# Talking-heads attention before two dense networks: four PSUM banks and an earlier place for the premix, scores in two banks one pair of heads a step

## The chip, the cores and the metric

The kernel runs on one NeuronCore of a Trainium2 chip. TensorE (PE in the rows) multiplies matrices into PSUM, VectorE (DVE), ScalarE (ACT) and GpSimd (POOL) work beside it, and SyncE (SP) issues the transfers, which 16 DMA engines carry out. The metric is the time of one execution on the device in microseconds (us), the median of several.

## The reference

Everything is float32. The attention mixes the heads twice, before and after the softmax; then come two dense networks.

```python
def _attn_ref(q, k, v, w_pre, w_post):            # q, k, v: (4, 12, 448, 64)
    scores = (1 / sqrt(64)) * matmul(q, k^T)      # (4, 12, 448, 448)
    scores = einsum('bhij,hg->bgij', scores, w_pre)
    scores = scores - max(scores, axis=-1)
    attn = exp(scores)
    attn = attn / (sum(attn, axis=-1) + 1e-09)
    attn = einsum('bhij,hg->bgij', attn, w_post)
    return matmul(attn, v)

x = attn_out.transpose(0, 2, 1, 3).reshape(1792, 768)
x = ((x @ w1) * (x @ w2)) @ w3 @ w_out            # _moe_ref
h = x @ w_in; out = maximum(0.01 * h, h) @ w_out2 # _moe2_ref
```

## The kernel before

`attention()` runs first, `moe()` after it. The attention takes, for each of the 4 batches, the 448 query rows in chunks of 120, 120, 120 and 88, and a chunk in blocks of ten rows: 12, 12, 12 and 9 blocks, 180 in all. A block's ten rows times twelve heads fill 120 partitions. This is how a block passes through:

- *Scores* (`qk`): for a pair of heads, `p`, six matmuls with queries and keys split in a high and a low half, into two PSUM banks `pq` (tag `qa`, four banks). ScalarE copies them to `s` (in the first two chunks VectorE copies one of the two), and after every second pair a transfer writes `s` to memory (`sdr`). Scores are made two chunks ahead (`QAHEAD`), in the steps listed in `QT`, two pairs a step.
- *Relayout* (`relayout`): a transfer reads a pair of blocks back as `sr`, with row and head on the partitions, eight steps ahead (`AHEAD`); there are five `sr` buffers.
- *Premix and softmax* (`premix`): for two blocks at once four matmuls mix the heads of `sr` into banks `pm` (one for each block, two in all); in the trace these are eight records. For each block VectorE takes the maximum `mx`, and ScalarE the exponential `e` with its sum.
- *Weights of the second mix* (`sums`, `weigh`): GpSimd adds 1e-9, VectorE takes the reciprocal `rc`, GpSimd scales the mixing matrix by it (`kr`), a step later.
- *Post-mix* (`postmix`): three steps later (`LAG`) four matmuls (eight records) mix `e` into `po` (two banks), and VectorE, or ScalarE in some steps, copies it to `ap`.
- *Values* (`av`): when a chunk's `ap` is full, at steps 3 and 4 of the next chunk, 24 matmuls (48 records) into `px`, a bank of tag `qa`, copied to `y` and written out.

Beside that, in steps that are not `plain` (those in `QT` or `AT`), `filler` advances: it converts a weight of the dense networks from a 64-bit format in 16 units of six calls, five operations on VectorE and two on ScalarE a unit, with one transfer in and one out. `lows` are the low halves of later queries and keys; their subtraction runs in steps 3 and 4 on VectorE, behind the post-mix's copy.

The attention is under a manual schedule: every engine gets its instructions in the order in which the loop over `n` at the end of `attention()` calls these functions, one step for each `n`, and runs them in that order. In a step this is: stores of the step before (`flush`), premix and softmax, `weigh`, `sums`, `relayout`, scores, `av`, post-mix, `lows`, filler. A PSUM tile of a tag takes the tag's banks in turn and waits until the one it gets has been read.

Of the kernel before, what the change touches and what calls it, by code (L numbers as in the profile page):

```python
# [23 lines left out]
def attention_moe_kernel(ctx: ExitStack, tc, qt, kt, vt, w_pre, w_post, w1, w2, w3t, w_out, w_in2, w_out2, out):  # L24
# [20 lines left out]
    HP = 2  # L45
# [21 lines left out]
    make_identity(nc, ident)  # L67

    ps = ctx.enter_context(tc.tile_pool(name="ps", bufs=2, space=PSUM))
    banks = {"qa": 4, "pm": 2, "po": 2}  # L70

    def bank(tag, shape, name):
        return ps.tile(shape, F32, tag=tag, name=name, bufs=banks[tag])
# [45 lines left out]
    def attention():  # L119
        with ExitStack() as es:  # L120
# [78 lines left out]
            def qk(b, c, p):  # L199

                m = cols[c]
                g, r = divmod(p, HP)
                first = (b, c) == order[0]
                if first and p == 0:
                    st[b, c] = late.tile([CH, H, S], F32, tag="ap", name="s", bufs=2)
                elif not first and r == 0:
                    st[b, c] = big.tile([CH, 2 * HP, S], F32, tag="s", name="s", bufs=4)
                t = st[b, c][:, 2 * g * HP:2 * (g + 1) * HP] if first else st[b, c]
                pq = [bank("qa", [CH, S], "pq") for _ in range(2)]
                for j, (x, y) in enumerate(((0, 0), (0, 1), (1, 0))):  # L210
                    for e in range(2):
                        rows = slice(e * D, (e + 1) * D)
                        nc.tensor.matmul(  # L213
                            pq[e][:m], qst[b, c][rows, p, x, :m], kst[b, p][rows, y, :], start=(j == 0), stop=(j == 2)
                        )
                for e in range(2):
                    if e and order.index((b, c)) < QAHEAD:
                        nc.vector.tensor_copy(t[:m, 2 * r + e, :], pq[e][:m])
                    else:
                        nc.scalar.activation(out=t[:m, 2 * r + e, :], in_=pq[e][:m], func=ACTF.Copy)  # L220
                if r == HP - 1:
                    stores.append((sdr[b, c][:, 2 * g * HP:2 * (g + 1) * HP, :], t[:m]))
# [30 lines left out]
                        nc.sync.dma_start(out=sr[s * Q:s * Q + HR, g], in_=st[b, c][q0:q0 + HQ])  # L253

            def premix(n):
                if n in srt:
                    sr = srt.pop(n)
                    for s, m, _, nb in pair_of(n):
                        pms[m] = bank("pm", [P, S], "pm")
                        rows = slice(s * Q, s * Q + nb // 2 * H)  # L260
                        for g in range(2):
                            nc.tensor.matmul(  # L262
                                pms[m][g * Q:(g + 1) * Q], kpre[rows], sr[rows, g, :], start=True, stop=True
                            )
                pm = pms.pop(n)
                mx = wk.tile([P, 1], F32, tag="mx", name="mx")
                nc.vector.tensor_reduce(out=mx, in_=pm, axis=AX.X, op=ALU.max, negate=True)  # L267
# [138 lines left out]
            for n in range(4, AHEAD):  # L406
                relayout(n)
            q_split(0, 2)()
            for n in range(NB + LAG):
                flush()  # L410
                plain = True
                if n < NB:
                    b, c, t, _ = blocks[n]
                    ci = order.index((b, c))
                    QT = (5, 8, 10) if ci == 0 else (0, 6, 9) if len(chunks[c][2]) > 9 else (0, 5, 7)
                    plain = t not in QT and t not in AT
                    premix(n)
                if 0 < n <= NB:
                    weigh(n - 1)
                if n < NB:  # L420
# [8 lines left out]
                        if c == NC - 2:  # L429
                            lows += [k_split(b + 1, p) for p in ((2, 3) if t == LAG else (4, 5))]  # L430
                    if ci + QAHEAD < len(order) and t in QT:
                        for r in range(HP):
                            qk(*order[ci + QAHEAD], HP * QT.index(t) + r)
                m = n - LAG
                if m >= 0:
                    tt = blocks[m][2]
                    if tt < 2 and m > tt:
                        av(*blocks[m - tt - 1][:2], tt)
                    postmix(m, nc.scalar.copy if n >= NB or plain and t in (1, 5, 8, 10) else nc.vector.tensor_copy)
                while lows:  # L440
                    lows.pop(0)()
                if n < NB:
# [16 lines left out]
    def moe():  # L459
        with ExitStack() as es:  # L460
# [4 lines left out]
            so = es.enter_context(tc.tile_pool(name="m_so", bufs=4, reuse_waits="tile"))  # L465
            wk = es.enter_context(tc.tile_pool(name="m_wk", bufs=2, reuse_waits="tile"))
            xp = es.enter_context(tc.tile_pool(name="m_x", bufs=1, reuse_waits="tile"))
            tags = itertools.cycle(("qa", "pm", "qa", "po"))

            def pst(shape, name):  # L470
                return bank(next(tags), shape, name)
# [219 lines left out]
```

## Time and profile before

| | us |
|---|---|
| median of 3 runs | 1470.07 |
| lowest, highest | 1465.48, 1473.9 |
| the profiled execution | 1471.89 |
| its span, first to last instruction | 1470.1 |

| share of the span | busy |
|---|---|
| TensorE matmuls | 94% |
| TensorE weight loads | 79% |
| VectorE | 59% |
| ScalarE | 42% |
| GpSimd | 10% |

The granted TensorE clock was 0.964 of full speed in the mean. The trace names the function's lines: L213 is `qk`'s matmul, L262 the premix's, L267 and L270 its maximum and exponential, L299 the post-mix's matmul, L306 its copy, L319 `av`'s matmul, L220 and L218 the copies of scores, L97 to L106 and `hl` the conversions. The attention fills the first 590 us, so views of a stretch say more than the page's totals. An engine's instructions are busy from start to end; matmuls are pipelined, so the next start is the better measure of what one costs.

### The profile page before, as it was taken

To read this page: it belongs to the slowest core of one execution; us is meant where nothing else is said; L and a number is where in the kernel's file an instruction comes from. 1 tells how busy PE (TensorE), PEld (TensorE's weight loads), DVE (VectorE), ACT (ScalarE), POOL (GpSimd) and SP (SyncE) were. 2 spreads that over 40 slices of the span, in tenths; PEclk is the share of its full clock that TensorE was granted. 3 is DMA by queue.
4 is the path that set the end of the run, shared out by engine and by line. 5 is a ranking of instruction groups with operands and counts; after the bars stand their busy time and mean duration, and the time that the engine had idled before them with its cause. 6 is when DMAs were issued, how large, how long until landed. Compare 5 with 4: busy or idle time off the path is not lost.

```text
span 1470.1 us, 23122 instructions
## 1 busy us (share of the span) xinstructions
PE 1388.4 (94%) x8880; PEld 1165.1 (79%) x8880; DVE 869.5 (59%) x1508; ACT 610.1 (42%) x1174; POOL 149.7 (10%) x371
## 2 busy tenths in 40 slices
PE   6788888898889998999999999999999999999998
PEld 3466565675566666998889899999988888999998
DVE  4344554545445456767643768687666446776962
ACT  3354555445454444533322445234333223552430
POOL 1222222222222232000000000000000000000000
PEclk8798999889889999999999999999999999999999
DMA  5965797677577687763314243242723131532401
GB/s 170 280 211 162 222 280 210 168 222 222 166 209 213 172 244 215 234 193 102 109 43 122 70 167 108 86 150 87 236 87 101 57 122 65 172 102 93 131 20 76
DMA packets 138861, 224.21 MB, mean 153 GB/s; under 512 B 20032, under 2 KB 120384, under 8 KB 138304
## 3 DMA queue, kind: packets, MB, share of 16 engines
q1 hardware_dynamic: 138752, 222.73, 50.3%
q8 instruction: 71, 1.16, 0.3%
q14 instruction: 38, 0.31, 0.1%
HBM read 162.86 MB, written 58.98 MB: 151 GB/s over the span
## 4 chain that ended last, share of the span: by engine, by line
PE 85%; DVE 5%; ACT 4%; issue 3%; DMA 2%; SPq 1%; DVEq 0%; ACTq 0%
PE pm L557 40%; PE po L626 16%; PE po L299 8%; PE pm L262 6%; PE px L319 6%; PE pq L213 5%; PE pw L495 5%; ACT e L270 3%; DVE mx L267 2%; DMA sr<-sdr 1%; DVE ap L306 1%; DMA sr<-s 1%; DVE ks L179 1%; DVE wc L103 1%; SPq L253 0%
## 5 line engine op out<-in xcount | busy, mean ns | idle before, releaser
L557 PE MATMUL pm<-x,ws 128*128 128x512 f32 (+1 forms) x2304 | 466.8, 363 | 0.0
L557 PEld LDWEIGHTS pm<-x,ws 128*128 128x128 f32 x2304 | 417.6, 188 | 47.7
L626 PE MATMUL po<-ws,g 128*128 128x384 f32 x1344 | 234.2, 334 | 0.0
L626 PEld LDWEIGHTS po<-ws,g 128*128 128x128 f32 x1344 | 233.1, 188 | 0.0
L270 ACT ACTIVATE e<-pm,mx 128x448 f32<-128x448 f32 x180 | 114.4, 635 | 254.3 <-DVE rc L282 236.0
L299 PEld LDWEIGHTS po<-kr,e 128*112 128x112 f32 x1440 | 166.9, 187 | 59.9 <-issue 31.7
L262 PE MATMUL pm<-sr,kpre 60*64 60x448 f32 x720 | 152.5, 574 | 53.6 <-ACT e L270 39.7
L299 PE MATMUL po<-kr,e 128*112 128x120 f32 (+1 forms) x1440 | 190.9, 285 | 1.8 <-ACT ap L306 1.8
L306 DVE COPY ap<-po 112x480 f32<-112x480 f32 (+1 forms) x125 | 81.4, 651 | 167.7 <-PE po L299 167.7
L79 DVE TENSOR_TENSOR ws<-wc,ws 128x768 fp32r<-128x768 f32 (+1 forms) x104 | 101.2, 975 | 76.8 <-ACT ws L76 76.4
L284 POOL TENSOR_SCALAR kr<-kpost,rc 128x120 f32<-128x120 f32 x180 | 105.7, 587 | 377.0 <-DVE rc L282 342.7
L95 ACT ACTIVATE wc<-wr 128x768 f32<-128x768 f32 (+2 forms) x120 | 104.5, 875 | 76.0 <-DVE ws L79 63.6
L76 ACT ACTIVATE ws<-wc 128x768 fp32r<-128x768 f32 (+1 forms) x104 | 89.1, 859 | 106.8 <-PE po L626 73.9
L267 DVE TENSOR_REDUCE mx<-pm 128x1 f32<-128x448 f32 x180 | 110.6, 616 | 36.3 <-PE pm L262 28.8
L262 PEld LDWEIGHTS pm<-sr,kpre 60*64 60x64 f32 x720 | 31.4, 133 | 113.7 <-ACT e L270 83.9
L557 PE MATMUL pm<-h,ws 128*128 128x512 f32 (+1 forms) x576 | 116.3, 363 | 0.0
L557 PEld LDWEIGHTS pm<-h,ws 128*128 128x128 f32 x576 | 104.3, 188 | 11.7
L319 PEld LDWEIGHTS px<-ap,vs 112*64 112x64 f32 x1536 | 91.0, 159 | 25.9 <-issue 25.1
L103 DVE SCALAR_TENSOR_TENSOR wc<-wr,wc 128x768 uint32<-128x768 uint32 (+2 forms) x120 | 109.9, 917 | 1.5
L106 DVE SCALAR_TENSOR_TENSOR wc<-wr,wc 128x768 uint32<-128x768 uint32 (+2 forms) x120 | 109.9, 916 | 1.2
L319 PE MATMUL px<-ap,vs 112*64 112x120 f32 (+1 forms) x1536 | 98.0, 294 | 12.7 <-DVE ap L306 9.0
L220 ACT ACTIVATE s<-pq 120x448 f32<-120x448 f32 (+1 forms) x180 | 84.5, 547 | 22.6 <-PE pq L213 21.8
(51 smaller groups left out, 1011.7 us busy)
## 6 DMA issues: line engine op xcount, KB each, us to landing
sr<-sdr SPq DMA_DIRECT2D x172, 210.0 KB
sdr<-s SPq DMA_DIRECT2D x36, 840.0 KB
wr<-in_moe_w_dram SPq DMA_DIRECT2D x32, 768.0 KB
wr<-in_moe_w_in_dram SPq DMA_DIRECT2D x32, 768.0 KB
wr<-in_moe_w_out_dram SPq DMA_DIRECT2D x32, 768.0 KB
wr<-in_moe_w_dram SPq DMA_DIRECT2D x8, 1024.0 KB
sdr<-s SPq DMA_DIRECT2D x12, 616.0 KB
wr<-in_moe_w_out_dram SPq DMA_DIRECT2D x16, 384.0 KB
```

Of the source, the lines that this page charges most:

```text
L79: nc.vector.tensor_tensor(out=dst, in0=src, in1=hi.bitcast(F32), op=ALU.subtract)
L95: nc.scalar.activation(out=cf, in_=hi.bitcast(F32), func=ACTF.Abs)
L103: lambda: nc.vector.scalar_tensor_tensor(out=c, in0=hi, scalar=0xC0000000, in1=c, op0=ALU.bitwise_and, op1=ALU.bitwise_or),
L106: lambda: nc.vector.scalar_tensor_tensor(out=c, in0=lo, scalar=29, in1=c, op0=ALU.logical_shift_right, op1=ALU.bitwise_or),
L262: nc.tensor.matmul(pms[m][g * Q:(g + 1) * Q], kpre[rows], sr[rows, g, :], start=True, stop=True)
L267: nc.vector.tensor_reduce(out=mx, in_=pm, axis=AX.X, op=ALU.max, negate=True)
L270: ends["act"] = nc.scalar.activation(out=e, in_=pm, func=ACTF.Exp, bias=mx, scale=1.0, accum_out=sm)
L284: ends["pool"] = nc.gpsimd.tensor_scalar(out=kr, in0=kpost, scalar1=rc, scalar2=None, op0=ALU.mult)
L299: nc.tensor.matmul(po[:, jc].rearrange("p h (g i) -> p h g i", g=2), e[:, jc * JP:(jc + 1) * JP], kr, start=True, stop=True,)
L319: nc.tensor.matmul(px[e * D:(e + 1) * D, p - p0, :ni], vst[b][:, jc, 2 * p + e, :], ap[:, jc, 2 * p + e, :ni], start=(jc == 0), stop=(jc = ...
L557: nc.tensor.matmul(dst, wt[:, a, kk, :], x[:, kk, c, c0:c0 + w], start=(kk == 0 and j == 0), stop=(kk == kn - 1 and j == 2),)
L626: nc.tensor.matmul(po, g[:, m, a, t * P:(t + 1) * P], wts[m][:, c, 0, cs], start=(m == 0 and j == 0), stop=(m == FQ - 1 and j == 2),)
```

## The change

The banks are dealt anew: `pm` gets four and `qa` two. The premix is taken apart: `premix` keeps the matmuls, and a new `softmax` has the maximum and the exponential. The matmuls of the next pair of blocks are issued at the end of an even step, behind the post-mix; the first pair's before the loop. Scores are made one pair of heads a step, in six steps of a chunk instead of three, and those of the first two chunks take `pm` banks for two pairs of three. With `QT` longer, there are more steps that are not plain: `filler` is called two times in each `QT` step, so 14 times a chunk instead of 8. The post-mix's copy is ScalarE's in all plain steps. In `moe()` the tags are dealt in another turn.

```diff
--- before.py
+++ after.py
@@ -67,7 +67,7 @@
     make_identity(nc, ident)
 
     ps = ctx.enter_context(tc.tile_pool(name="ps", bufs=2, space=PSUM))
-    banks = {"qa": 4, "pm": 2, "po": 2}
+    banks = {"qa": 2, "pm": 4, "po": 2}
 
     def bank(tag, shape, name):
         return ps.tile(shape, F32, tag=tag, name=name, bufs=banks[tag])
@@ -206,7 +206,7 @@
                 elif not first and r == 0:
                     st[b, c] = big.tile([CH, 2 * HP, S], F32, tag="s", name="s", bufs=4)
                 t = st[b, c][:, 2 * g * HP:2 * (g + 1) * HP] if first else st[b, c]
-                pq = [bank("qa", [CH, S], "pq") for _ in range(2)]
+                pq = [bank("pm" if (b, c) in order[:QAHEAD] and p % 3 else "qa", [CH, S], "pq") for _ in range(2)]
                 for j, (x, y) in enumerate(((0, 0), (0, 1), (1, 0))):
                     for e in range(2):
                         rows = slice(e * D, (e + 1) * D)
@@ -253,6 +253,7 @@
                         nc.sync.dma_start(out=sr[s * Q:s * Q + HR, g], in_=st[b, c][q0:q0 + HQ])
 
             def premix(n):
+
                 if n in srt:
                     sr = srt.pop(n)
                     for s, m, _, nb in pair_of(n):
@@ -262,6 +263,8 @@
                             nc.tensor.matmul(
                                 pms[m][g * Q:(g + 1) * Q], kpre[rows], sr[rows, g, :], start=True, stop=True
                             )
+
+            def softmax(n):
                 pm = pms.pop(n)
                 mx = wk.tile([P, 1], F32, tag="mx", name="mx")
                 nc.vector.tensor_reduce(out=mx, in_=pm, axis=AX.X, op=ALU.max, negate=True)
@@ -406,15 +409,17 @@
             for n in range(4, AHEAD):
                 relayout(n)
             q_split(0, 2)()
+            premix(0)
             for n in range(NB + LAG):
                 flush()
                 plain = True
                 if n < NB:
                     b, c, t, _ = blocks[n]
                     ci = order.index((b, c))
-                    QT = (5, 8, 10) if ci == 0 else (0, 6, 9) if len(chunks[c][2]) > 9 else (0, 5, 7)
+                    nt = len(chunks[c][2])
+                    QT = (5, 7, 8, 9, 10, 11) if ci == 0 else (0, 1, 5, 7, 9, 11) if nt > 9 else (0, 1, 2, 5, 7, 8)
                     plain = t not in QT and t not in AT
-                    premix(n)
+                    softmax(n)
                 if 0 < n <= NB:
                     weigh(n - 1)
                 if n < NB:
@@ -429,14 +434,15 @@
                         if c == NC - 2:
                             lows += [k_split(b + 1, p) for p in ((2, 3) if t == LAG else (4, 5))]
                     if ci + QAHEAD < len(order) and t in QT:
-                        for r in range(HP):
-                            qk(*order[ci + QAHEAD], HP * QT.index(t) + r)
+                        qk(*order[ci + QAHEAD], QT.index(t))
                 m = n - LAG
                 if m >= 0:
                     tt = blocks[m][2]
                     if tt < 2 and m > tt:
                         av(*blocks[m - tt - 1][:2], tt)
-                    postmix(m, nc.scalar.copy if n >= NB or plain and t in (1, 5, 8, 10) else nc.vector.tensor_copy)
+                    postmix(m, nc.scalar.copy if n >= NB or plain else nc.vector.tensor_copy)
+                if n < NB and t % 2 == 0:
+                    premix(n + len(pair_of(n)))
                 while lows:
                     lows.pop(0)()
                 if n < NB:
@@ -465,7 +471,7 @@
             so = es.enter_context(tc.tile_pool(name="m_so", bufs=4, reuse_waits="tile"))
             wk = es.enter_context(tc.tile_pool(name="m_wk", bufs=2, reuse_waits="tile"))
             xp = es.enter_context(tc.tile_pool(name="m_x", bufs=1, reuse_waits="tile"))
-            tags = itertools.cycle(("qa", "pm", "qa", "po"))
+            tags = itertools.cycle(("pm", "qa", "pm", "po"))
 
             def pst(shape, name):
                 return bank(next(tags), shape, name)
```

Three places in the engines' order. The first is TensorE in the middle of a chunk of twelve blocks, the third of the second batch, from its second `px` on (step 4). Before:

```order
L319 MATMUL px<-ap,vs 64x120 x24
L299 MATMUL po<-kr,e 112x120 x8
L262 MATMUL pm<-sr,kpre 64x448 x4
L213 MATMUL pq<-ks,qs 120x448 x12
L299 MATMUL po<-kr,e 112x120 x8
L262 MATMUL pm<-sr,kpre 64x448 x4
L299 MATMUL po<-kr,e 112x120 x4
L213 MATMUL pq<-ks,qs 120x448 x12
L299 MATMUL po<-kr,e 112x120 x4
L262 MATMUL pm<-sr,kpre 64x448 x4
```

After:

```order
L322 MATMUL px<-ap,vs 64x120 x24
L302 MATMUL po<-kr,e 112x120 x4
L263 MATMUL pm<-sr,kpre 64x448 x4
L213 MATMUL pq<-ks,qs 120x448 x6
L302 MATMUL po<-kr,e 112x120 x8
L263 MATMUL pm<-sr,kpre 64x448 x4
L213 MATMUL pq<-ks,qs 120x448 x6
L302 MATMUL po<-kr,e 112x120 x8
L263 MATMUL pm<-sr,kpre 64x448 x4
L213 MATMUL pq<-ks,qs 120x448 x6
L302 MATMUL po<-kr,e 112x120 x8
L263 MATMUL pm<-sr,kpre 64x448 x4
```

A group of twelve score matmuls has become two of six, two steps apart, and the premix, which stood a step later behind one post-mix more, follows the post-mix of an even step.

The second is ScalarE's order where one chunk ends and the next begins (88 columns: scores for a chunk of nine blocks; 120: the next). Before:

```order
L220 ACTIVATE s<-pq 88x448 x4
L270 ACTIVATE e,sm<-pm,mx 128x448
L306 COPY ap<-po 112x48x10
L270 ACTIVATE e,sm<-pm,mx 128x448 x2
L220 ACTIVATE s<-pq 120x448 x4
L95 ACTIVATE wc<-wr 128x384
L270 ACTIVATE e,sm<-pm,mx 128x448
L306 COPY ap<-po 112x48x10
```

After:

```order
L309 COPY ap<-po 112x48x10
L273 ACTIVATE e,sm<-pm,mx 128x448
L220 ACTIVATE s<-pq 88x448 x2
L76 ACTIVATE hl<-wc 128x384
L273 ACTIVATE e,sm<-pm,mx 128x448
L220 ACTIVATE s<-pq 120x448 x2
L273 ACTIVATE e,sm<-pm,mx 128x448
L220 ACTIVATE s<-pq 120x448 x2
L95 ACTIVATE wc<-wr 128x384
L273 ACTIVATE e,sm<-pm,mx 128x448
L309 COPY ap<-po 112x48x10
```

There are now score copies in three steps that follow each other, the last of a chunk and the first two of the next, each between two exponentials; before there were two steps without any between them.

The third is VectorE at the end of a chunk in the first batch, with conversions (`wc`, `hl`). Before:

```order
L306 COPY ap<-po 112x48x10
L267 TENSOR_REDUCE mx<-pm 128x1
L282 RECIPROCAL rc<-sm 128x1
L306 COPY ap<-po 112x48x10
L100 TENSOR_SCALAR wc<-wc 128x384
L103 SCALAR_TENSOR_TENSOR wc<-wr,wc 128x384
L267 TENSOR_REDUCE mx<-pm 128x1
L282 RECIPROCAL rc<-sm 128x1
L267 TENSOR_REDUCE mx<-pm 128x1
L282 RECIPROCAL rc<-sm 128x1
L306 COPY ap<-po 112x48x10
```

After:

```order
L79 TENSOR_TENSOR hl<-wc,hl 128x384
L97 TENSOR_SCALAR wc<-wc 128x384
L270 TENSOR_REDUCE mx<-pm 128x1
L285 RECIPROCAL rc<-sm 128x1
L309 COPY ap<-po 112x48x10
L100 TENSOR_SCALAR wc<-wc 128x384
L103 SCALAR_TENSOR_TENSOR wc<-wr,wc 128x384
L270 TENSOR_REDUCE mx<-pm 128x1
L285 RECIPROCAL rc<-sm 128x1
L309 COPY ap<-po 112x48x10
L106 SCALAR_TENSOR_TENSOR wc<-wr,wc 128x384
L270 TENSOR_REDUCE mx<-pm 128x1
```

Behind each `ap` of a step with scores there are now one or two conversions before the next `mx`, in steps that follow each other; before, one step of the same stretch had them.

## Rows read from the trace of the kernel before

**Rows 1.** Busy time by stretch: us, each engine's busy time (instructions), clock, DMA share, GB/s

```profile
50.00:550.00 500.00, 448.95 (x3828) 307.37 (x3827) 245.76 (x584) 246.32 (x610) 134.25 (x330) 0.92 0.74 211
...
600.00:650.00 50.00, 50.00 (x290) 50.00 (x289) 39.61 (x48) 23.85 (x36) 0.00 (x0) 1.00 0.73 236
```

**Rows 2.** TensorE by line, 50 to 550 us: count, busy and mean, idle before, releasers

```profile
L299 PE MATMUL po<-kr,e 128*112 128x120 f32 (+1 forms) x1320 | 175.3, 285 | 0.0
L262 PE MATMUL pm<-sr,kpre 60*64 60x448 f32 (+1 forms) x660 | 133.4, 564 | 39.7 <-ACT e L270 38.9
L319 PE MATMUL px<-ap,vs 112*64 112x120 f32 (+1 forms) x1344 | 88.8, 300 | 11.3 <-DVE ap L306 8.1 <-issue 3.2
L213 PE MATMUL pq<-ks,qs 64*120 64x448 f32 (+1 forms) x504 | 69.3, 412 | 0.0
```

**Rows 3.** TensorE in time: start, duration, instruction, count, idle before and its releaser

```profile
62.26 1.89 PE L299 MATMUL po<-kr,e 128*112 128x120 f32 x16
64.08 0.97 PE L262 MATMUL pm<-sr,kpre 60*64 60x448 f32 x4
66.07 0.97 PE L262 MATMUL pm<-sr,kpre 60*64 60x448 f32 x4 [1.02 <-ACT e L270]
66.97 1.48 PE L213 MATMUL pq<-ks,qs 64*120 64x448 f32 x12
68.38 1.89 PE L299 MATMUL po<-kr,e 128*112 128x120 f32 x16
...
161.33 0.98 PE L262 MATMUL pm<-sr,kpre 60*64 60x448 f32 x8
162.25 2.68 PE L319 MATMUL px<-ap,vs 112*64 112x120 f32 x48
164.86 1.07 PE L299 MATMUL po<-kr,e 128*112 128x120 f32 x8
165.86 1.47 PE L213 MATMUL pq<-ks,qs 64*120 64x448 f32 x12
```

**Rows 4.** TensorE in time after a longer wait, and the stretch's busy times and clock

```profile
266.75 1.28 PE L262 MATMUL pm<-sr,kpre 60*64 60x448 f32 x4 [1.47 <-ACT e L270]
267.97 2.60 PE L213 MATMUL pq<-ks,qs 64*120 64x448 f32 x12
...
270.00:280.00 10.00, 9.69 (x60) 6.67 (x60) 4.21 (x11) 5.58 (x15) 2.43 (x6) 0.79 0.71 191
```

**Rows 5.** All engines in time, one post-mix and what follows it

```profile
302.44 1.07 PE L299 MATMUL po<-kr,e 128*112 128x120 f32 x8
...
303.55 0.66 DVE L306 COPY ap<-po 112x480 f32<-112x480 f32 x1 [0.46 <-PE po L299]
...
304.39 0.62 DVE L267 TENSOR_REDUCE mx<-pm 128x1 f32<-128x448 f32 x1
...
305.13 0.63 ACT L270 ACTIVATE e<-pm,mx 128x448 f32<-128x448 f32 x1 [2.81 <-DVE rc L282]
...
305.75 1.83 ACT L220 ACTIVATE s<-pq 120x448 f32<-120x448 f32 x4
```

**Rows 6.** VectorE by line, 50 to 550 us: two of the conversions

```profile
L103 DVE SCALAR_TENSOR_TENSOR wc<-wr,wc 128x384 uint32<-128x384 uint32 x16 | 8.9, 556 | 0.4
...
L97 DVE TENSOR_SCALAR wc<-wc 128x384 f32<-128x384 f32 x16 | 5.6, 352 | 0.0
```

**Rows 7.** Busy time by stretch, where transfers are dense, and two lines of transfer issues

```profile
50.00:60.00 10.00, 9.60 (x58) 6.87 (x57) 4.74 (x11) 4.39 (x12) 2.86 (x8) 0.72 1.05 227
60.00:70.00 10.00, 8.98 (x67) 5.88 (x68) 4.04 (x10) 6.41 (x15) 2.63 (x7) 1.00 0.97 290
320.00:330.00 10.00, 9.26 (x129) 8.02 (x128) 4.17 (x10) 2.56 (x8) 2.17 (x6) 0.83 1.01 295
...
wr<-in_moe_w_out_dram SPq DMA_DIRECT2D x16, 384.0 KB
wos<-hl SPq DMA_DIRECT2D x16, 384.0 KB
```

## The prediction

> **What bounds the kernel now.** I read the busy time by stretch first. From 600 us on TensorE is busy for all 50 of 50 us at full clock, and that part, the two dense networks, is left alone by the change; only its bank names are dealt anew, and a bank of each name is still used again after eight tiles. So the question is the attention, some 590 us. In 500 us of it [rows 1] TensorE is busy 449 us, VectorE and ScalarE 246 each, the granted clock is 0.92 and the transfers take 0.74 of their engines. TensorE is the engine to look at, and it idles only 51 us.
>
> Then its lines in that stretch [rows 2]: 1320 matmuls of the post-mix are 165 blocks at 8 records each, so a block takes 3.03 us. 39 us of the idle time stand before the premix (`pm`), nearly all ended by ScalarE's exponential `e`, and 11 before `px`.
>
> Third, TensorE in order of time [rows 3]. The first five rows are one pair of blocks: two post-mixes start 1.82 us apart from the premix, whose first half runs 0.97 us alone, then 1.02 us of waiting for `e`, then the second half. The loop is plain: two `pm` banks hold both blocks of a pair, the next pair's premix needs them empty, and both maxima and exponentials lie between. The other rows of the group show it undisturbed: eight records together start the next work after 0.92 us. So a split premix costs 0.95 us that the profile calls busy.
>
> The Trainium skill says the same of the counter ("Perfetto Trace Analysis", Identifying the Most-Contended Engine: matmul busy time is a poor measure of the distance to the roofline). By busy time alone the change could give back 51 us at most, a time of about 1421; the sum below goes by starts in the rows instead.
>
> What the matmuls of the stretch would take end to end at full clock, from starts [rows 3] and counts [rows 2]:
> - post-mix: 165 blocks at 0.91 in twos and 1.00 alone, 0.95 taken: 157 us
> - premix: 82.5 pairs at 0.92: 76
> - scores: 504/12 = 42 groups at 1.41: 59
> - `px`: 1344/48 = 28 at 2.61: 73
>
> Together 365 us, 2.21 a block. Of the 500 us, 51 are idle. The premix is busy 133.4 us; 82.5 pairs of 0.98 would be 81, and 52 over 0.97 says that some 54 pairs ran split: 51 us. The 33 left (449 - 365 - 51) are the clock: after 1.47 us of idling the same twelve score matmuls took 2.60 us, against 1.48, with 0.79 granted in that stretch [rows 3, 4], a time spent partly at the 1.2 GHz level and otherwise at 2.4.
>
> **The change part by part.** *Premix ahead.* The premix of a pair now stands at the end of the even step before it and needs the exponentials of blocks that the other engines had two steps earlier. From the end of a post-mix to `e` is 0.04 + 0.66 (`ap`) + 0.62 (`mx`) + 0.12 + 0.62 = 2.1 us [rows 5], while TensorE has two post-mixes, a premix and mostly half a score group, over 2.7 us, before it asks. So the wait and the split go: 39 + 51 us. The premix also slips between the last post-mix and `px`, so the waits there, 11 us in all, are covered. If that cover failed, they would be paid again, nothing more. The new risk is data: the premix is now ahead of a post-mix in TensorE's queue and would hold it up if `sr` had not landed. The load is issued six to seven steps ahead instead of eight, about 17 us instead of 24. In the 500 us no idle time of size is ended by it [rows 2], so I take nothing here and put the risk with the transfers below.
>
> *Scores in two banks, a pair a step.* The work is the same, 84 steps of 6 matmuls instead of 42 of 12. What is new is that two banks hold just one pair, so each step needs ScalarE's two copies of the step before it to be done. Where a step without scores lies between, there is time enough. Where two score steps follow each other there isn't. From the end of a post-mix: 0.04, `ap` 0.66, `mx` 0.62, 0.12, `e` 0.62, two copies at 0.46 each (four took 1.83), 0.04 make 3.0 us [rows 5]. TensorE meanwhile has a premix 0.92, half a score group 0.71 and a post-mix 0.95, 2.6 in all: a wait of 0.5. With two conversion steps between `ap` and `mx`, 0.35 to 0.56 each [rows 6], 0.8 in all, the wait is 1.3 us. All that stands behind the waiting score matmul, the post-mix and then `ap`, `mx` and `e` of the next blocks, is held up too, so it costs in full. Six steps in a chunk make 36 such neighbours in 14 chunks: four in the first chunk, two in each of the others with twelve blocks, four in each with nine. 16 have conversions: 16 x 1.3 + 20 x 0.5 = 31 us. Bounds: 0 if ScalarE keeps up, and 84 x 1.3 = 109 if every step waited.
>
> *Conversions sooner.* They run in steps that have scores, now twice as many: 14 calls a chunk instead of 8, so the 98 calls are done by about block 92, not in the twelfth chunk. No work is added, but it lies on fewer blocks. At the two `px` steps of a chunk VectorE also has low halves to subtract, two operations like the 0.56 one [rows 6]; I take 0.8 us a chunk for 15 chunks, 12 us (bounds 0 and 24).
>
> *Copies.* `ap` goes to ScalarE in 52 steps instead of 55, three more VectorE copies at 0.66: 2 us on an engine half idle, nothing. *The start.* The first scores get six banks instead of four. From 50 us on the transfers are at 1.05 of their share [rows 7] and the premixes there wait for data, so I take 0 (bounds -3 and 3).
>
> *Transfers.* 211 GB/s for 500 us are 105 MB, 0.64 MB a block, of which the conversions' 16 loads and 16 stores of 384 KB are 12.6 MB. Without them 0.56 MB a block; with all of them in 78 blocks 0.73 there. The rows with a share near 1 moved 227, 290 and 295 GB/s [rows 7], 271 in the mean: 2.69 us a block. By the terms above the engines need 2.21 + 29/78 of waits + 0.12 of clock = 2.70 in those blocks, so both are at their limits together. I add 8 us for that (bounds 0 and 41, from 290 and from 227 GB/s).
>
> *Clock.* Waits fall from 51 + 51 to 31 + 12. In proportion the 33 us become 14 (bounds 0 and 33).
>
> The sum for the stretch: 365 + 31 + 12 + 14 + 8 = 430 us instead of 500, 70 less. The nine blocks behind it lose the split and the waits too (102/165 a block) but have no scores, less the 12 us kind: 3 us. The profiled execution took 1471.9 us (span 1470.1), 1.8 above the median of 1470.07, well within the runs. 1471.9 - 73 = 1399; the median lies a little lower, so I say 1398.
>
> **The rivals.**
> 1. *TensorE runs dense.* ScalarE and VectorE catch up during the two `px` steps and no score step waits; the clock then stays up. 31 + 12 + 14 + 8 fall away: 1335 to 1360. For it: both engines are busy half the time. Against it: the order on VectorE ties `mx` to the post-mix before it.
> 2. *Transfers set the pace of the first half.* At 227 GB/s a block takes 3.22 us, at 248 2.94, against 2.80 in the forecast: 11 to 33 us more, 1409 to 1431. For it: rows at a share of 1 already [rows 7]. Against it: they are bursts, and pairs are loaded many steps ahead.
> 3. *The clock doesn't recover.* The short waits before scores keep it at 0.92 and the 33 us stay: 1417. The rows bear it out so far: 1.47 us of idling was followed by a lower clock [rows 3, 4]. The Trainium skill ("TensorE: Matmul & The Clock Gate", A second HAM failure mode) describes short idle times while cycling through PSUM banks that set the clock swinging.
> 4. *No gain.* VectorE falls so far behind that the premix still waits for `e`, one step later than now: 1465 to 1478.
> 5. *Slower: the two score banks become the loop.* ScalarE's queue is late in all score steps, not only neighbours, since `ap` copies and `e` alternate with score copies there. Without score waits the sum is 1367; the time of before returns at 103/84 = 1.2 us for each of the 84 steps. With the 0.56 us lag of a late ScalarE copy added to 1.3 it is 1.9 each, 160 us: 1527. For it: no second pair of banks. Against it: in alternate steps the copies have a whole step of 2 us more.
>
> **How the numbers follow.** Forecast (1380 to 1412) 0.46; dense 0.13; transfers 0.16; clock 0.09; no gain 0.06; slower 0.10. About 0.5% is what a measurement of this kernel can tell from no change. Faster by more than that 0.84, within it 0.06, slower 0.10. The range leaves out the slower case, no gain, and the lower part of the dense case: 1352 to 1435.
>
> **What would show it.** Right: `pm` no longer waits for `e`, its busy time falls to about 80 us for as many pairs, and idle time before `pq` ended by ScalarE's score copies appears, about 30 us, at chunk ends. The first half shows a transfer share of 0.9 or more, and blocks are slower there than after the conversions. Wrong: idle time before `pm` ended by `sr` transfers (rival 2), a clock still at 0.92 (rival 3), `pq` idle over 80 us (rival 5), or hardly any (rival 1).

## The result, and the profile after

| | before | after |
|---|---|---|
| median of four runs, us | 1468.38 | 1384.45 |
| lowest to highest, us | 1465.48 to 1473.9 | 1381.86 to 1387.82 |
| the profiled execution, us | 1471.89 | 1382.40 |
| its span, us | 1470.1 | 1380.6 |

The changed kernel takes 0.9426 of the time of before (95% interval 0.9387 to 0.9464): 84 us less by the medians, 89.5 by the two profiled spans. The prediction was 1398 with a range of 1352 to 1435 and a gain of 73 us against the profiled execution.

All of it is in the attention. The first matmul of the dense networks started at 584.97 us before and starts at 495.45 now, 89.5 us earlier, which is the whole difference of the spans. The first rows are the busy time by stretch, in the columns of [rows 1]:

```profile
50.00:470.00 420.00, 398.40 (x3920) 279.07 (x3922) 254.24 (x604) 243.94 (x621) 158.61 (x342) 0.99 0.86 255
...
50.00:300.00 250.00, 234.16 (x2258) 163.82 (x2258) 160.64 (x381) 149.81 (x377) 97.88 (x192) 0.98 0.88 267
300.00:470.00 170.00, 164.24 (x1667) 115.25 (x1668) 93.60 (x224) 94.13 (x244) 60.73 (x150) 1.00 0.84 237
```

TensorE is busy 398 of 420 us where it was 449 of 500 [rows 1], the granted clock is 0.99 instead of 0.92, and the transfers are at 0.86 instead of 0.74 of their engines: much the same bytes in less time. The second and third row part the stretch near where the conversions end (the last `hl` is written at 281 us). The lines of TensorE in it, which answer [rows 2]:

```profile
L302 PE MATMUL po<-kr,e 128*112 128x120 f32 (+1 forms) x1368 | 173.6, 276 | 0.1
L263 PE MATMUL pm<-sr,kpre 60*64 60x448 f32 (+1 forms) x684 | 89.4, 561 | 0.8 <-DMA sr<-sdr 0.6
L213 PE MATMUL pq<-ks,qs 64*120 64x448 f32 (+1 forms) x504 | 81.1, 396 | 6.9 <-ACT s L220 6.3
L322 PE MATMUL px<-ap,vs 112*64 112x120 f32 (+1 forms) x1364 | 75.0, 268 | 13.8 <-ACT ap L309 12.9 <-ACT s L220 0.9
```

The premix `pm` waits 0.8 us where it waited 39.7, and none of that for `e`. Its 684 records are 85.5 pairs, 89.4 us, 1.05 us a pair; before it was 133.4 us for 82.5 pairs, 1.62. So the split is gone as well as the wait. What is idle now, 21.6 us, stands before `px` (13.8) and before the scores `pq` (6.9). TensorE in time, one end of a chunk and the next one's beginning, in the columns of [rows 3]:

```profile
97.00 1.07 PE L302 MATMUL po<-kr,e 128*112 128x120 f32 x8
98.92 1.30 PE L213 MATMUL pq<-ks,qs 64*120 64x448 f32 x6 [0.85 <-ACT s L220]
100.15 1.08 PE L302 MATMUL po<-kr,e 128*112 128x120 f32 x8
101.16 0.98 PE L263 MATMUL pm<-sr,kpre 60*64 60x448 f32 x8
102.07 0.87 PE L213 MATMUL pq<-ks,qs 64*120 64x448 f32 x6
102.87 1.90 PE L302 MATMUL po<-kr,e 128*112 128x120 f32 x16
104.70 0.98 PE L263 MATMUL pm<-sr,kpre 60*64 60x448 f32 x8
107.26 2.68 PE L322 MATMUL px<-ap,vs 112*64 112x120 f32 x48 [1.58 <-ACT ap L309]
```

The score step at 98.92 us waits 0.85 us for ScalarE's score copies of the step before, and then runs 1.30 us instead of 0.87, because its second bank comes free only in the middle of it. The next score step, at 102.07, doesn't wait at all, though it too follows a step with scores; before it a premix lies between (101.16), before 98.92 a post-mix alone. And the premix at 104.70 stands between the last post-mix and `px`, as foreseen, but `px` still waits 1.58 us behind it.

### The profile page after: what moved, and what is told of

The parts are those of the page before. It is cut to its first block, busy times and chain, and to the rows that moved or that the text cites. A ratio compares the mean times of both kernels' runs of the same rounds, so it can differ in the third digit from the quotient of the medians.

```text
span 1380.6 us, 22898 instructions
## 1 busy us (share of the span) xinstructions
PE 1327.5 (96%) x8880; PEld 1130.8 (82%) x8880; DVE 871.0 (63%) x1511; ACT 602.2 (44%) x1171; POOL 169.0 (12%) x371
## 4 chain that ended last, share of the span: by engine, by line
PE 87%; DMA 4%; ACT 4%; DVE 2%; issue 1%; SPq 1%; POOL 0%; DVEq 0%; ACTq 0%
PE pm L563 42%; PE po L632 17%; PE po L302 9%; PE px L322 6%; PE pw L501 5%; PE pq L213 4%; PE pm L263 4%; DMA sr<-sdr 2%; ACT e L273 2%; DMA wos<-hl 1%; DVE mx L270 1%; ACT ap L309 1%; DMA sr<-s 1%; ACT s L220 1%; SPq L253 0%
## 5 line engine op out<-in xcount | busy, mean ns | idle before, releaser
L302 PEld LDWEIGHTS po<-kr,e 128*112 128x112 f32 x1440 | 158.8, 179 | 41.7 <-issue 31.9
L302 PE MATMUL po<-kr,e 128*112 128x120 f32 (+1 forms) x1440 | 183.1, 277 | 1.9 <-ACT ap L309 1.6
L309 DVE COPY ap<-po 112x480 f32<-112x480 f32 x128 | 84.1, 657 | 101.6 <-PE po L302 100.5
L287 POOL TENSOR_SCALAR kr<-kpost,rc 128x120 f32<-128x120 f32 x180 | 113.4, 630 | 267.8 <-DVE rc L285 222.6
L263 PE MATMUL pm<-sr,kpre 60*64 60x448 f32 x720 | 104.3, 573 | 17.2 <-DMA sr<-sdr 9.9
L270 DVE TENSOR_REDUCE mx<-pm 128x1 f32<-128x448 f32 x180 | 109.9, 614 | 13.8 <-PE pm L263 13.8
L213 PEld LDWEIGHTS pq<-ks,qs 64*120 64x120 f32 (+1 forms) x576 | 49.9, 180 | 75.2 <-ACT s L220 32.8
L213 PE MATMUL pq<-ks,qs 64*120 64x448 f32 (+1 forms) x576 | 94.2, 410 | 14.3 <-ACT s L220 6.3
L322 PEld LDWEIGHTS px<-ap,vs 112*64 112x64 f32 x1536 | 78.6, 144 | 27.8 <-ACT ap L309 22.2
L322 PE MATMUL px<-ap,vs 112*64 112x120 f32 (+1 forms) x1536 | 85.5, 271 | 14.4 <-ACT ap L309 13.5
```

Source lines behind the costliest of these rows:

```text
L213: nc.tensor.matmul(pq[e][:m], qst[b, c][rows, p, x, :m], kst[b, p][rows, y, :], start=(j == 0), stop=(j == 2))
L263: nc.tensor.matmul(pms[m][g * Q:(g + 1) * Q], kpre[rows], sr[rows, g, :], start=True, stop=True)
L287: ends["pool"] = nc.gpsimd.tensor_scalar(out=kr, in0=kpost, scalar1=rc, scalar2=None, op0=ALU.mult)
L302: nc.tensor.matmul(po[:, jc].rearrange("p h (g i) -> p h g i", g=2), e[:, jc * JP:(jc + 1) * JP], kr, start=True, stop=True,)
L322: nc.tensor.matmul(px[e * D:(e + 1) * D, p - p0, :ni], vst[b][:, jc, 2 * p + e, :], ap[:, jc, 2 * p + e, :ni], start=(jc == 0), stop=(jc = ...
```

## The experiments

Each gives a ratio to the time of before, measured on the same chip and with the same runs of before beside it. Their medians lay between 1468 and 1473 us, so where two kernels of different experiments are close, the difference of the ratios stands beside that of the medians.

**The place of the premix without the banks.** In the kernel before, `premix` was parted and its matmuls moved as in the change; nothing else.

```diff
-                    premix(n)
+                    softmax(n)
...
+                if n < NB and t % 2 == 0:
+                    premix(n + len(pair_of(n)))
```

> The kernel before with the premix issued at the end of the even step before, and nothing else: pm keeps two banks, scores four banks and two pairs a step. Theory A, the banks free TensorE: the premix now asks for banks whose exponentials belong to the step in progress and the next one, with one post-mix less in front of it, so each of some 83 pairs waits about 0.9 us longer than before: about 1545 us, slower than before, with idle time before pm ended by e well above 40 us. Rival B, the earlier place is what counts: half the gain or more without the banks, 1430 us or less.

1672.05 us, 1.1338 of before (0.9426 for the whole change). Line of `pm` and the busy times of the stretch:

```profile
L262 PE MATMUL pm<-sr,kpre 60*64 60x448 f32 (+1 forms) x688 | 194.8, 660 | 132.3 <-ACT e L271 130.5
...
50.00:770.00 720.00, 587.55 (x4016) 381.52 (x4015) 254.52 (x608) 254.69 (x626) 139.75 (x344) 0.80 0.56 155
```

The earlier place alone is a large loss. `pm` now waits 132 us instead of 39.7: with two banks the premix needs the exponential of a step that hasn't begun, and the post-mix that could have been done meanwhile stands behind it in TensorE's queue. Theory A held in its direction and was 127 us short. The clock is the rest: 0.80 granted in this stretch, so TensorE's busy time grew from 449 to 588 us for 173 blocks instead of 165.

**The banks without the place.** In the changed kernel the premix went back to the start of its own step.

```diff
-            premix(0)
...
+                    premix(n)
                     softmax(n)
...
-                if n < NB and t % 2 == 0:
-                    premix(n + len(pair_of(n)))
```

> The changed kernel with the premix put back to the start of its own step, ahead of its maximum; four pm banks, two score banks and the six score steps stay. Theory A: no wait of pm for e and no split premix, as in the changed kernel; only the premix no longer lies between the last post-mix and px, so some 0.9 us more are idle there in 15 chunks: about 1398 us. Rival B: the maxima now wait for a premix in TensorE's queue, the loop is as tight as before: 1440 us or more.

1391.29 us, 0.9438 (0.9406 to 0.9470), within the interval of the whole change (7 us slower by the medians, 2 by the ratios).

```profile
L263 PE MATMUL pm<-sr,kpre 60*64 60x448 f32 (+1 forms) x660 | 82.5, 562 | 0.0
L322 PE MATMUL px<-ap,vs 112*64 112x120 f32 (+1 forms) x1344 | 74.3, 269 | 19.4 <-ACT ap L309 15.4 <-ACT s L220 2.4 <-DVE ap L309 1.7
```

No wait before `pm`, no split; 19.4 us before `px` instead of 13.8. So nearly all of the gain comes without the earlier place, from the two banks with the scores spread as they are; the place gives a few microseconds, if anything. In the two traces they show before `px` and in the post-mixes: with a premix or scores between them, nearly all stand alone here, at 1.00 us to the next start instead of 1.82 for two, and the 165 blocks spend 168 us in them instead of 160. Not run was the changed kernel with two `pm` banks and its scores spread; the next experiment comes nearest to it.

**Three and three.** The same eight banks, dealt `qa` 3, `pm` 3.

```diff
-    banks = {"qa": 2, "pm": 4, "po": 2}
+    banks = {"qa": 3, "pm": 3, "po": 2}
```

> The changed kernel with three banks for the premix and three for scores. Theory: a pair's second premix now needs the exponential of the step in progress, which ends about 2.1 us behind a post-mix against 1.7 us of other work: a wait of 0.5 to 1 us and a split premix for most of 83 pairs, 1450 to 1500 us, with idle time before pm ended by e of 40 us or more; waits before pq go. Rival, three banks are as good as four: 1375 to 1390 us.

1453.20 us, 0.9855 (0.9827 to 0.9883).

```profile
L263 PE MATMUL pm<-sr,kpre 60*64 60x448 f32 (+1 forms) x678 | 142.9, 567 | 33.7 <-ACT e L273 33.2
L213 PE MATMUL pq<-ks,qs 64*120 64x448 f32 (+1 forms) x504 | 78.3, 411 | 0.9 <-ACT s L220 0.9
```

Waits before scores are nearly gone (0.9 us), but `pm` waits 33.7 us for `e` and runs 142.9 us for 85 pairs, 1.69 each: split again. With three banks the second premix of a pair needs the exponential of the step in progress. By the ratios the fourth bank, taken from the scores, is worth 63 us; a third for scores is worth some 6 of waiting.

**Scores two pairs a step.** Two score banks, but three score steps with two pairs each, as before the change; conversions and copies kept their steps.

```diff
-                        qk(*order[ci + QAHEAD], QT.index(t))
+                        for r in range(HP):
+                            qk(*order[ci + QAHEAD], HP * ST.index(t) + r)
```

> The changed kernel with scores made two pairs a step in three steps, as before, but with two banks; conversions and copies keep their steps. Theory: the second pair of a step needs ScalarE's copies of the first, which stand behind the exponential of that step: 42 waits of 1.5 to 2 us, 1445 to 1470 us, idle before pq ended by ScalarE's score copies of 60 us or more. Rival, ScalarE keeps up and the spreading of scores is worth nothing: 1380 to 1390 us.

1498.61 us, 1.0175 (1.0134 to 1.0215): a little slower than before. The line of `pq`, one score step in time with ScalarE's work (TensorE's score matmuls, two exponentials, a copy of `ap`, the score copies), and the busy times:

```profile
L213 PE MATMUL pq<-ks,qs 64*120 64x448 f32 (+1 forms) x504 | 93.6, 412 | 80.3 <-ACT s L220 80.3
...
301.56 0.48 PEld L213 LDWEIGHTS pq<-ks,qs 64*120 64x120 f32 x6 [0.70 <-issue]
...
302.10 0.63 ACT L273 ACTIVATE e<-pm,mx 128x448 f32<-128x448 f32 x1 [3.49 <-DVE rc L285]
...
302.72 0.56 ACT L309 COPY ap<-po 112x480 f32<-112x480 f32 x1
...
303.17 0.64 ACT L273 ACTIVATE e<-pm,mx 128x448 f32<-128x448 f32 x1
...
303.78 0.98 ACT L220 ACTIVATE s<-pq 120x448 f32<-120x448 f32 x2
...
304.38 1.30 PE L213 MATMUL pq<-ks,qs 64*120 64x448 f32 x6 [1.96 <-ACT s L220]
...
50.00:600.00 550.00, 453.55 (x4074) 311.34 (x4072) 261.89 (x624) 257.26 (x635) 157.50 (x353) 0.93 0.73 203
```

The second pair waits 1.96 us: the first pair's copies stand behind the step's exponentials. 80.3 us are idle before `pq` in 42 steps, 1.9 each, in the range I gave for each. The time is 29 us above my range all the same: 0.43 us more each are lost when the second bank comes late (1.30 instead of 0.87), and the clock is 0.93 again, both of which I had left out. Without the spreading into six steps the four premix banks would have cost more than they gave: the two parts of the change belong together.

**Other score steps.** No scores in a chunk's last step, so that its last and the next one's first are no neighbours; step 2 of a chunk of twelve has scores, which puts its post-mix copy on VectorE.

```diff
-(0, 1, 5, 7, 9, 11) if nt > 9 else (0, 1, 2, 5, 7, 8)
+(0, 2, 5, 6, 8, 10) if nt > 9 else (0, 1, 2, 5, 6, 7)
```

> The changed kernel with the score steps moved: 0, 2, 5, 6, 8, 10 in chunks of twelve blocks and 0, 1, 2, 5, 6, 7 in those of nine, so that the last step of a chunk has none. Step 2 thereby has its post-mix copy on VectorE. Theory: the waits before scores come where a chunk's last step and the next one's first both have scores; without that neighbour and with the copy of step 2 on VectorE both the 14 us before px and about 10 of the 13 us before pq go: 1360 to 1368 us. Rival, the neighbours 5 and 6 pay what 11 and 0 paid: 1370 to 1376 us, only the copy's gain.

1375.76 us, 0.9329 (0.9303 to 0.9355).

```profile
114.38 0.86 PE L213 MATMUL pq<-ks,qs 64*120 64x448 f32 x6
115.17 1.07 PE L302 MATMUL po<-kr,e 128*112 128x120 f32 x8
117.87 1.88 PE L213 MATMUL pq<-ks,qs 64*120 64x448 f32 x6 [1.62 <-ACT s L220]
...
127.26 0.87 PE L213 MATMUL pq<-ks,qs 64*120 64x448 f32 x6
...
L213 PE MATMUL pq<-ks,qs 64*120 64x448 f32 (+1 forms) x504 | 82.0, 399 | 9.5 <-ACT s L220 9.4
L322 PE MATMUL px<-ap,vs 112*64 112x120 f32 (+1 forms) x1436 | 76.4, 263 | 0.1
```

The rival was right. Steps 5 and 6 are neighbours now, with one post-mix and no premix between them, and the second of them waits 1.62 us at 117.87; the scores at 127.26, alone, don't. 9.5 us are idle before `pq`, more than the 6.9 of the change. What was gained is the wait before `px`: 0.1 us. Of these 14 us the time shows 9 (14 by the ratios). In the trace the 165 blocks spend 167 us in post-mixes instead of 160, since with these score steps nearly all of them stand alone.

**The copy of step 2.** Only that part: VectorE copies the last post-mix that `px` needs.

```diff
-nc.scalar.copy if n >= NB or plain else nc.vector.tensor_copy
+nc.scalar.copy if n >= NB or plain and t != 2 else nc.vector.tensor_copy
```

> The changed kernel with the post-mix copy of step 2 (the last one that px needs) on VectorE instead of ScalarE. Theory: the 14 us idle before px come from that copy standing on ScalarE behind the step's exponential; on VectorE it ends within the premix that lies ahead of px: 10 to 14 us less, 1370 to 1375 us. Rival, the wait is TensorE's lead and only moves to the next score or premix: 1383 to 1386 us.

1373.87 us, 0.9309 (0.9282 to 0.9336), 11 us better than the change by the medians, 17 by the ratios.

```profile
L213 PE MATMUL pq<-ks,qs 64*120 64x448 f32 (+1 forms) x504 | 81.1, 396 | 7.2 <-ACT s L220 6.6
L322 PE MATMUL px<-ap,vs 112*64 112x120 f32 (+1 forms) x1440 | 77.3, 263 | 7.6 <-DVE ap L309 4.1 <-issue 3.0 <-ACT s L220 0.5
```

The wait before `px` falls from 13.8 to 7.6 us, and that before scores stays (7.2): 6 us of it were the copy's place on ScalarE, behind the exponential, and they did not come back elsewhere. The other 7.6 stay, over half of them now ended by VectorE's copy. The idle time saved is about half of the gain by the medians; in the trace `px` also ran 2 us shorter, without the lower clock that the next experiment shows.

**One conversion call.** As before the change, one call a score step instead of two.

```diff
-                        for _ in range(2 if n >= START and t in QT else 1):
+                        for _ in range(1):
```

> The changed kernel with one conversion call in a score step instead of two, so 8 a chunk as before the change, spread over twelve chunks. The prediction's step: two conversions behind a copy lengthen the chain by 0.8 us where scores wait; with one it is 0.4 in twice as many chunks, and the transfer share of the first half falls from 0.88 to about 0.82. If transfers held the first half up: 8 us or more faster, 1376 us or less. If only the chain counts: within 4 us of the changed kernel.

1373.81 us, 0.9331 (0.9305 to 0.9357): 11 us better by the medians, 14 by the ratios, more than the chain would give. Of the two causes I had named neither shows: no matmul waits for a transfer of any size, and the transfer share from 50 to 300 us is 0.88 as in the change. The trace of the change shows a third one. All engines in time, and the stretch around:

```profile
191.29 0.66 DVE L309 COPY ap<-po 112x480 f32<-112x480 f32 x1 [0.97 <-PE po L302]
191.81 0.52 ACT L76 ACTIVATE hl<-wc 128x384 fp32r<-128x384 f32 x1 [2.57 <-DMA wos<-hl]
192.00 1.96 PE L263 MATMUL pm<-sr,kpre 60*64 60x448 f32 x8
192.23 0.62 ACT L273 ACTIVATE e<-pm,mx 128x448 f32<-128x448 f32 x1
...
192.99 0.19 PEld L263 LDWEIGHTS pm<-sr,kpre 60*64 60x64 f32 x4 [0.80 <-ACT e L273]
...
194.46 0.56 ACT L309 COPY ap<-po 112x480 f32<-112x480 f32 x1
...
195.07 4.30 PE L322 MATMUL px<-ap,vs 112*64 112x120 f32 x48 [1.11 <-ACT ap L309]
...
160.00:200.00 40.00, 36.13 (x353) 26.00 (x352) 22.14 (x54) 21.98 (x56) 15.59 (x30) 0.91 0.90 285
```

ScalarE has to write the high half `hl` (191.81) and stands 2.57 us until the transfer that stores the previous `hl` has landed; there is one `hl` tile. Behind it wait the exponential (192.23), for that the second half of the premix (its weights load at 192.99, and the premix takes 1.96 us in two parts) and the copy of `ap` (194.46), for that `px` (195.07, 1.11 us idle), and then `px` takes 4.30 us instead of 2.68: from 196 to 199 us 0.50 of the clock was granted, the 1.2 GHz level. A like fall (0.50 from 166 to 168 us) follows a wait of 1.91 us before the `px` at 164.27, with a wait of `hl` ahead of it (1.1 us); together they are the 0.91 from 160 to 200 us. Such waits of `hl` are 8.3 us, five in all. With one call a step there are none, and the same stretch has the full clock:

```profile
160.00:200.00 40.00, 37.52 (x426) 27.44 (x426) 24.70 (x60) 22.08 (x57) 15.06 (x31) 1.00 0.94 288
```

**Two tiles for `hl`.** The cause by itself: a second `hl` tile (and two `wc` instead of three, for room), two calls a step.

```diff
-F32R, tag="hl", name="hl", bufs=1)
+F32R, tag="hl", name="hl", bufs=2)
...
-convert_steps(ws, t, (1, n), 3)
+convert_steps(ws, t, (1, n), 2)
```

> The changed kernel with two hl tiles instead of one (and two wc tiles instead of three, to make room), two conversion calls in a score step. Theory: what two calls cost is ScalarE standing before hl until the transfer that stores the last hl has landed (8 us in 5 waits), with the exponential and the score copies behind it: 8 to 11 us faster, 1373 to 1377 us, and no wait of hl for that store. Rival, it is VectorE's longer chain or the transfers themselves: 1382 to 1386 us.

1376.72 us, 0.9356 (0.9330 to 0.9383); the wait of `hl` for the store is gone.

```profile
L213 PE MATMUL pq<-ks,qs 64*120 64x448 f32 (+1 forms) x504 | 81.0, 396 | 7.0 <-ACT s L220 6.4
L322 PE MATMUL px<-ap,vs 112*64 112x120 f32 (+1 forms) x1392 | 75.5, 266 | 12.4 <-ACT ap L309 12.4
```

So the single tile is a cause, worth about 8 us by the medians and 10 by the ratios, though the two profiled executions are only 3.7 us apart, and the intervals hardly part. The idle times before `pq` and `px` are near those of the change (7.0 and 12.4); what the traces show is mostly `px` without the lower clock, 2.5 us in all.

**Both cures.** The copy of step 2 together with one call a step, and together with two `hl` tiles.

> The changed kernel with both the copy of step 2 on VectorE and one conversion call in a score step. If the two have separate causes (the wait before px; ScalarE held up by conversions), the gains of about 10 us each add up: 1362 to 1367 us. Rival, both take the same waits away: 1372 to 1375 us.

> The changed kernel with the copy of step 2 on VectorE and two hl tiles (two wc), two conversion calls a score step. If the store of hl is what two calls cost, this is as fast as one call with the copy moved, 1362 to 1367 us; if the conversions' density itself costs, it stays at 1371 to 1375 us.

1371.09 us, 0.9319 (0.9290 to 0.9348), and 1369.97 us, 0.9315 (0.9285 to 0.9345): by the ratios no better than the copy alone, by the medians 3 and 4 us, which is within the intervals. TensorE's lines of the second:

```profile
L213 PE MATMUL pq<-ks,qs 64*120 64x448 f32 (+1 forms) x498 | 80.0, 396 | 7.2 <-ACT s L220 6.6
L322 PE MATMUL px<-ap,vs 112*64 112x120 f32 (+1 forms) x1440 | 76.9, 263 | 6.3 <-DVE ap L309 4.1 <-issue 2.2
```

They are nearly those of the copy alone: 7.2 and 6.3 us idle. Whether the gains add is left open. By the times they don't, or not wholly. In the traces the dense networks start 8.0 us earlier than in the change with the copy alone, 3.7 with two tiles and 12.4 with both, which is about their sum; with one call they start 8.3 us earlier, and 10.4 with that and the copy. One part can be had only once: with the copy alone the late `hl` still waits 8.9 us, but no stretch of 20 us from 60 to 480 us has less than the full clock. The best kernels run are the copy alone and these two, at 0.931 to 0.932.

**More work on VectorE.** One more operation behind the post-mix copy in each score step.

```diff
+                    if n >= START and t in QT and ci + QAHEAD < len(order):
+                        nc.vector.tensor_scalar(out=pad, in0=pad, scalar1=1.0, scalar2=None, op0=ALU.mult)
```

> The changed kernel with one more VectorE operation (a multiplication of a 128x448 tile by one, into itself, about 0.4 to 0.6 us) at the end of each score step from step 14 on, so on all of some 78 score steps, between a post-mix copy and the next maximum. Theory: a chunk pays only where scores of neighbouring steps wait, once in two steps and not at each, some 20 places, the rest has slack: 8 to 14 us slower, 1392 to 1398 us. Rival, VectorE is at its limit: 78 times 0.5, 35 us or more slower, 1420 us and above.

1394.94 us, 0.9475 (0.9436 to 0.9515), 10 us above the change by the medians and 7 by the ratios, whose intervals overlap.

```profile
54.00:470.00 416.00, 385.33 (x3760) 270.24 (x3757) 263.78 (x649) 234.22 (x594) 169.67 (x319) 0.98 0.82 243
...
PE px L323 <- ACT ap L310: 16.1, 11, 2.8
...
PE pq L214 <- ACT s L221: 10.8, 15, 1.3
```

The waits before scores went from 6.3 to 10.8 us and those before `px` from 12.9 to 16.1. The trace has 76 of the added operations, 0.38 us each, 29 us in all. VectorE isn't the bound; its extra work is paid where a score step or `px` waits, and has slack elsewhere.

**The start.** All scores of the first two chunks in the two `qa` banks.

```diff
-bank("pm" if (b, c) in order[:QAHEAD] and p % 3 else "qa", [CH, S], "pq")
+bank("qa", [CH, S], "pq")
```

> The changed kernel with all scores of the first two chunks in the two qa banks instead of six banks in turn. Theory: the start is set by the loads of sr, which wait for stores of the scores, so later scores come out later one to one: twelve pairs with two banks each wait about 0.5 to 1 us for their copies, 6 to 12 us slower, 1391 to 1397 us. Rival, the transfers of the start hide it: 1384 us, no change.

1388.66 us, 0.9422 (0.9397 to 0.9447): 4 us slower than the change by the medians, no difference by the ratios. The traces show the start, first of the change and then of this run:

```profile
47.28 2.57 PE L263 MATMUL pm<-sr,kpre 60*64 60x448 f32 x8 [9.23 <-DMA sr<-sdr]
49.77 3.24 PE L302 MATMUL po<-kr,e 128*112 128x120 f32 x16
...
50.90 2.60 PE L263 MATMUL pm<-sr,kpre 60*64 60x448 f32 x8 [8.04 <-DMA sr<-sdr]
53.42 3.54 PE L302 MATMUL po<-kr,e 128*112 128x120 f32 x16
```

The premix waits for a load either way, but with two banks the load comes later, and the first post-mix starts 3.65 us later. So six banks at the start give some 4 us, less than the 6 to 12 of the theory and too little for the ratios to show.

## Why the prediction came out as it did

*Premix: right.* Wait and split went, 39 and some 50 us, and the experiments put it on the banks. The prediction gave the reason by the exponentials two steps back; with four banks that holds at the old place as well.

*Cover before `px`: wrong.* The step said that the premix would lie in the wait and cover it. It does lie there; but the change also put the copy of step 2, the one `px` waits for, on ScalarE behind that step's exponential, and 13.8 us are idle there where 0 were forecast. I had counted the copies that change engines (52 for 55, "nothing") and not asked who waits for which of them. The copy moved back measures it: 6.2 of the 13.8 us were its place. The other 7.6 weren't covered either; over half of them end with VectorE's copy, and what would take them away wasn't tested.

*Scores in two banks: the mechanism right, the places and their number wrong.* A wait at a first neighbour is 0.85 us and 0.43 in the second bank, 1.28 against the 1.3 of the sum; after the conversions it is 0.1 and 0.4, against 0.5. But the sum let all 36 neighbours pay, and gave TensorE a premix to do before each of them. In the trace there are two kinds. Before 18 of them a post-mix alone lies between the two groups of scores, as before 98.92: 16 of these wait, and in all 18 the second bank comes late. Before the other 18 a premix lies between as well, as before 102.07, and none waits. The chain also spans two steps, so that a wait at one neighbour gives the next its time; which of the two counts for more wasn't tested. As the price was worked out with the premix and is paid where there is none, its size is in part luck. 6.9 us idle and 81.1 busy, against 84 steps at 0.87, make 15 us, not 31.

*Low halves: 12 forecast.* What shows is about 5: `pm` is busy 89.4 us for 85.5 pairs of 0.98, and part of that is the wait of `hl`.

*Conversions and transfers: the term of 8 us for crowded transfers was not there.* From 50 to 300 us they moved 267 GB/s at a share of 0.88, as much as the prediction took for their limit, and no matmul waited more than 0.6 us for one. Blocks were slower while conversions ran, as foreseen (2.63 us each from block 2 to 92, 2.27 from there to block 166). Denser conversions did cost, through a single tile whose store had to land. The prediction looked at the bandwidth and not at what a transfer holds.

*Clock: 14 forecast, 0.99 granted.* Rival 3, by which waits before scores would keep it at 0.92, didn't come true: between 60 and 480 us the clock fell to the 1.2 GHz level twice, both times behind a wait before `px` (1.91 and 1.11 us), and was at 2.4 GHz otherwise. The Trainium skill ("TensorE: Matmul & The Clock Gate", A second HAM failure mode) describes a kernel whose frequent short idle times between groups of matmuls let the clock swing between its two levels. The experiments with more idle time fit that, with 0.80 and 0.93 granted in the mean; the change, with 21.6 us of it left, hardly shows it.

Counted by post-mixes (eight records a block), the 165 blocks from the second on took 407.5 us, from the start of one post-mix to that of another, instead of the 430 of the sum. Beside the 365 for the pieces these are 15 scores, 5 premix, 14 `px`, and 8.5 that are left. Smaller terms than forecast, 16 + 7 + 8 for scores, low halves and transfers and 5.5 for the clock, less the 14 that were missed, are that difference. But the 8.5 aren't all clock. A group of six scores takes 0.80 us to the next start (102.07 to 102.87), so two take 1.60 where one of twelve took 1.41 [rows 3]: 8 us over 42 of them, which the prediction put at nothing ("the work is the same"). Without idle time the pieces take 386.7 us in the change and 382.4 with the copy moved and two `hl` tiles, where the clock was whole, so the lower clock cost about 4. That terms too large and terms left out partly cancelled is luck.

The start came out 1.8 us later at the second block (0 forecast), and what follows the 165 blocks 1.6 us longer (3 shorter forecast). The last `px`, before and after:

```profile
579.67 3.86 PE L319 MATMUL px<-ap,vs 112*64 112x88 f32 x96 [0.57 <-ACT ap L306]
...
487.63 6.38 PE L322 MATMUL px<-ap,vs 112*64 112x88 f32 x96 [0.57 <-ACT ap L309]
```

It takes 2.5 us more, with 0.61 of the clock granted from 485 to 490 us and 0.76 to 496, where before it was whole. So the gain in the profile is 89.5 us, not 73.

Rival 5 was near: with two pairs a step its loop showed, 1498.61 us, 27 us above the time of before, where 57 were worked out for it. What kept it away is the spreading over six steps.

## What to carry to other kernels

Where PSUM is full, ask of each tag how many tiles are alive between the first write and the last read of a loop that another engine closes, and give the banks there; here four for the premix and two for the scores, with the scores spread, took 84 us off, and three and three only 20. The tag that loses banks must have its work spread until every refill falls behind its reader's copies, or the gain is lost. And when a copy changes engines, look at the one copy that something waits for, not at the number of copies.

## What was not expected

A tile that is the source of a store holds up the engine that writes it next until the store has landed: up to 2.57 us of ScalarE with one tile, none with two. Transfers at a share of 0.88 for 250 us, and 0.86 over 420 us, left matmuls waiting 0.6 us in all. And the clock came back nearly whole, 0.99, with 21.6 us of idle time still there, in some 30 waits of up to 1.91 us, while with 132 us in waits of up to 2.8 us it was 0.80. The length of a single wait does not settle it: 1.91 us before a `px` was followed by a fall of the clock, and 1.71 before another was not.
